# Sparse attention into two mixtures of experts on one core: local q and k loaded heads side by side and turned by 128-wide products, half of the strided v moved to GpSimd's queue

## The chip, the cores and the metric

The kernel runs on 1 core of one Trainium2 chip. The metric is the device time of one execution in microseconds, taken on that core. The median of 3 runs of the kernel before is 1208.98 us (1208.12 to 1211.52).

## What is computed

Three layers one after the other, in float32. Only the first is touched by the change. It is attention over 4 batches of 8 heads, 576 positions of 64 numbers each. Heads 0 to 3 look at the last 32 positions ("local"), heads 4 to 7 at the earlier positions of the same residue modulo 32 ("strided"):

```
scores = scale * np.matmul(q, k.transpose(0, 1, 3, 2))
rel = pos[:, None] - pos[None, :]
mask_local = (rel >= 0) & (rel < stride)
mask_strided = (rel >= 0) & (pos[None, :] % stride == pos[:, None] % stride)
masks = np.stack([mask_local if h < H // 2 else mask_strided for h in range(H)], axis=0)
...
attn = attn / (np.sum(attn, axis=-1, keepdims=True) + 1e-09)
return np.matmul(attn, v)
```

Its 2304 rows of 512 then go through a mixture of 8 experts with a fixed capacity of 288 rows each, and through a second one in which every row passes all 4 experts with given weights.

## The kernel before

`front` (L48) does the attention and the first router's logits; `experts` does the two mixtures and takes most of the time. In `front` the work of a batch is cut into 10 units: 5 strided ones (two groups of 6 or 7 residues times 18 positions each) and 5 local ones (blocks of 64 queries by 96 keys). Over the 4 batches these are 40 units. A loop over t (L374 on) works on several units at once, at a fixed distance: at step t the scores of unit t (`scores`, L186 strided, L189 local, both TensorE), the exponentials of t-1 (`exps`, L205, ScalarE), their normalisation for t-2 (`norm`, L213 and L214 on VectorE and the product L215 on GpSimd), the turning of the weights of t-4 (`tr_p`, L222 TensorE, then a copy by ScalarE into `pT`), and the product with v of t-5 (`av`, L235 strided from `vs`, L242 local from `vl`).

Before scores can be taken, q and k must have the head dimension on the partitions. `piece` does that, two pieces a step (`pre`), 16 pieces a batch. Strided pieces (L153) are four TensorE transposes of 72 rows into a PSUM tile `tr` and a copy into `qS` or `kS`. Local pieces (L164) are six products with the identity: three times t, two times x (the head of a pair), each with a 96x64 tile of `ql` or `kl` as the weights, the two heads written to partitions 0 to 63 and 64 to 127. One copy then moves 128x288 numbers to `qL` (VectorE and ScalarE by turns, scaled) or `kL` (VectorE); it reads PSUM in order and writes every sixth number of a row, because a partition of `ql` holds six consecutive positions. There are 8 local pieces a batch, 32 in all.

The order on each engine is the order in which the code is written; no scheduler moves it. `keep_busy` (L409) adds products of a constant tile in the first steps.

Loads go by SyncE's queue: at the start `load_qk(0)`, `load_v(0)`, `load_qk(1)` and `load_vl(0)`; then at each step t with t % 10 == 2 first `load_qk` of the batch after next and then `load_v` of the next batch, and at t % 10 == 6 `load_vl` of the next batch. `load_v` issues 13 transfers (L73) for the ten tiles of `vs`, `load_vl` five (L80, L82) for `vl`, `load_qk` one for each of `qs`, `ks`, `ql`, `kl` (L59, L62; the first batch has `qs` and `ks` in four slices). A transfer issued by SyncE waits until the one eight places earlier has landed, since eight semaphores go round. In the prologue GpSimd issues four small loads of its own (L110, L116, L119).

When the loop is over, `experts` writes the attention rows out (L282, L292), routes and gathers them, and runs its products.

Of the kernel before, what the change touches and what calls it, by code (L numbers as in the profile page):

```python
# [18 lines left out]
FT = mybir.dt.float32  # L19
# [15 lines left out]
def dap(t, off, *dims):  # L35
    return bass.AP(tensor=t.tensor, offset=t.offset + off, ap=[list(d) for d in dims])

def front(tc, ident, hot, q, k, v, wg, dp, xd, L, ready, hold, deferred):
    nc = tc.nc
    B, H, S, D = q.shape  # L40
    hs = S * D
    with ExitStack() as st:
        cst = st.enter_context(tc.tile_pool(name="fc", bufs=1))
        ld = st.enter_context(tc.tile_pool(name="fl", bufs=2))
# [6 lines left out]
        def load_qk(b, kinds="sl"):  # L51
            T = LD.setdefault(b, {})
            if "s" in kinds:
                for nm in ("qs", "ks"):
                    T[nm] = ld.tile([72, 32, 64], FT, name=nm)
            n = 8 if b == 0 else 32
            for r in range(0, 32 if "s" in kinds else 0, n):
                for nm, src in (("qs", q), ("ks", k)):
                    nc.sync.dma_start(T[nm][:, r:r + n].rearrange("p r d -> p (r d)"), dap(src, (b * H + 4) * hs + r * D, [hs, 4], [32 * D, 18], [1, n * D]))  # L59
            for nm, src in (("ql", q), ("kl", k)) if "l" in kinds else ():  # L60
                T[nm] = ld.tile([96, 4, 6, 64], FT, name=nm)
                nc.sync.dma_start(T[nm].rearrange("p h r d -> p h (r d)"), dap(src, b * H * hs, [6 * D, 96], [hs, 4], [1, 6 * D]))  # L62

        def load_v(b, lo=0, hi=10):
            T = LD[b]
            if not lo:
                T["vs"] = ld.tile([126, 10, 128], FT, name="vs")
            for t, (b0, n) in list(enumerate(zip(starts, sizes)))[lo:hi]:
                p = 0
                while p < n:  # L70
                    h, rp = divmod(b0 + p, 16)
                    m = min(n - p, 16 - rp)
                    nc.sync.dma_start(T["vs"][18 * p:18 * (p + m), t], dap(v, (b * H + 4 + h) * hs + 2 * rp * D, [2 * D, m], [32 * D, 18], [1, 2 * D]))  # L73
                    p += m

        def load_vl(b):
            T = LD[b]
            T["vl"] = ld.tile([96, 9, 256], FT, name="vl")
            nc.gpsimd.memset(T["vl"][:32, 0], 0.0)
            nc.sync.dma_start(T["vl"][32:, 0].rearrange("p (h d) -> p h d", d=D), dap(v, b * H * hs, [D, 64], [hs, 4], [1, D]))  # L80
            for h in range(4):
                nc.sync.dma_start(T["vl"][:, 1:, 64 * h:64 * h + 64], dap(v, (b * H + h) * hs + 32 * D, [D, 96], [64 * D, 8], [1, D]))  # L82

        load_qk(0)
        load_v(0, 0, 6)
        load_qk(1, "s")
        load_v(0, 6)
# [32 lines left out]
        units = []  # L120
# [7 lines left out]
        def copy(out, in_, scale=None, eng="p"):  # L128

            flip[0] += 1  # L130
            ch = side_of[eng]
            if ch == "a" or (ch == "f" and flip[0] % 2):
                if scale is None:
                    nc.scalar.copy(out, in_)
                else:
                    nc.scalar.activation(out, in_, AF.Copy, scale=scale)
            elif scale is None:
                nc.vector.tensor_copy(out, in_)
            else:
                nc.vector.tensor_scalar(out, in_, scale, None, op0=OP.mult)  # L140

        def piece(b, i):

            j, i = divmod(i, 8)
            p = ps.tile([128, 512], FT, name="tr", bufs=2)
            sc = 0.125 if j == 0 else None
            if i < 4:
                if i == 0:
                    (QS, KS)[j][b] = wk.tile([128, 4, 16, 18], FT, name=("qS", "kS")[j])
                src, dst = LD[b][("qs", "ks")[j]], (QS, KS)[j][b]  # L150
                for a in range(4):
                    r = 8 * i + 2 * a
                    nc.tensor.transpose(p[:, 72 * a:72 * a + 72], src[:, r:r + 2, :].rearrange("p r d -> p (r d)"), ident[:72, :72])  # L153
                copy(dst[:, :, 4 * i:4 * i + 4, :].rearrange("p h r j -> p r h j"), p[:, :288].rearrange("p (r h j) -> p r h j", r=4, h=4), sc, "q" if sc else "p")
            else:
                hp, a = divmod(i - 4, 2)
                if i == 4:
                    (QL, KL)[j][b] = wk.tile([128, 2, 576 + 32 * j], FT, name=("qL", "kL")[j])
                    if j:
                        nc.gpsimd.memset(KL[b][:, :, :32], 0.0)  # L160
                src, dst = LD[b][("ql", "kl")[j]], (QL, KL)[j][b]
                for t in range(3):
                    for x in range(2):
                        nc.tensor.matmul(p[64 * x:64 * x + 64, 96 * t:96 * t + 96], src[:, 2 * hp + x, 3 * a + t, :], ident[:96, :96], start=True, stop=True)  # L164
                copy(dst[:, hp, 32 * j:].rearrange("p (s a t) -> p a t s", a=2, t=3)[:, a], p[:, :288].rearrange("p (t s) -> p t s", t=3), sc, "q" if sc else "r")

        def shape(n):
            b, kind, g = units[n]
# [141 lines left out]
        def logits(n):  # L310
            b, kind, g = units[n]
            if kind or g not in (2, 4):
                return
            i0, m = (0, 128) if g == 2 else (128, 160)
            p = LP[n] = ps.tile([128, 512], FT, name="xr", bufs=2)
            for h in range(4):
                nc.tensor.matmul(p[32 * h:32 * h + 32, :m], wgs[:, h], XTS[b].rearrange("p h j r -> p h (j r)")[:, h, i0:i0 + m], start=True, stop=False)
            if n < N - 1:
                logits_local(n)
# [44 lines left out]
        p = ps.tile([128, 512], FT, name="pt")  # L364
# [9 lines left out]
        for t in range(N + 14):  # L374
            t_now[0] = t
            if t < N and t % 10 == 2 and units[t][0] + 1 < B:
                if units[t][0] + 2 < B:
                    load_qk(units[t][0] + 2)
                load_v(units[t][0] + 1)
                nxt = [(units[t][0] + 1, i) for i in ORDER]  # L380

            if t < N and t % 10 == 6 and units[t][0] + 1 < B:
                load_vl(units[t][0] + 1)
            if t == 28:
                side = cst.tile([128, 18, 8], FT, name="side")
                nc.gpsimd.memset(side, 0.0)
                nc.gpsimd.iota(side.bitcast(I32)[:, :, 4], pattern=[[1, 18]], base=0, channel_multiplier=18)
                rs = cst.tile([128, 18], FT, name="rs")
                nc.vector.tensor_reduce(rs, pr, AX.X, OP.add)
                nc.vector.tensor_scalar(rs, rs, 1e-9, None, op0=OP.add)  # L390
                nc.vector.reciprocal(rs, rs)
                nc.vector.tensor_tensor(side[:, :, :4], pr, rs[:, :, None].to_broadcast([128, 18, 4]), OP.mult)
                nc.gpsimd.dma_start(dap(xd, 512, [18 * XW, 128], [XW, 18], [1, 8]), side)
            if t % 10 == 6:
                todo += nxt
                nxt = []

            def at(d, f):
                if 0 <= t - d < N:
                    f(t - d)  # L400

            def pre():
                if todo and t:
                    piece(*todo.pop(0))

            def keep_busy(n):
                p = ps.tile([128, 512], FT, name="xr", bufs=2)
                for i in range(n):
                    nc.tensor.matmul(p, hot[:, :128], hot, start=True, stop=True)  # L409

            if BUSY[0] <= t < BUSY[1]:
                keep_busy(BUSY[2] + 2 * (t < 2))
            at(4, tr_p)
            if N < t < N + 5:
                keep_busy(2)
            at(2, norm)
            while late2:
                x = late2.pop(0)
                if x is None:
                    break  # L420
                x()
            while late:
                late.pop(0)()
            if t == N + 4:
                logits(N - 1)
            at(5, av)
            rows("o")
            if t < N:
                at(10, logits)
            elif t == N + 3:  # L430
                logits(N - 3)
            elif t == N + 5:
                logits_local(N - 1)
            pre()
            at(1, exps)
            rows("s")
            if t < N:
                scores(t)
            pre()
# [941 lines left out]
```

## Time and profile before

| what | value |
|---|---|
| median of 3 runs | 1208.98 us |
| the profiled execution, its own time | 1208.96 us |
| its span, first to last instruction | 1207.2 us |
| TensorE busy over the span | 1177.4 us (98%) |
| VectorE / ScalarE / GpSimd busy | 71% / 52% / 35% |
| the attention loop | about 11 to 125 us of the span |

The times of rows are microseconds from the span's start unless they say ns. A busy engine is not an engine at its peak: matmuls are pipelined and their ends are modelled. The share of the whole span says little about a change in the first tenth of it, so that tenth is read by itself below.

### The profile page before, as it was taken

The page shows a single profiled execution, that of the slowest core. Times are in us where ns is not written, and L with a number is a line of the kernel's source. Part 1 is how long each engine was busy: PE and PEld are TensorE (multiplying, and loading weights), DVE is VectorE, ACT ScalarE, POOL GpSimd, SP SyncE. Part 2 cuts the span into 40 slices and gives each one's busy share as a digit, 9 for nine tenths or more (in the row PEclk, how much of TensorE's full clock was granted, in tenths as well). Part 3 has the DMA queues.
Part 4 walks back from the last instruction along what each step waited for, and adds up shares of the span by engine and source line. Part 5 has one row for each costly group of instructions (what it writes and reads, how often), then busy time and mean ns, then how long its engine had stood idle before and what let it go on. Part 6 is the DMA issues. An engine that isn't in the chain of part 4 may idle for free.

```text
span 1207.2 us, 24909 instructions
## 1 busy us (share of the span) xinstructions
PE 1177.4 (98%) x9088; PEld 1038.6 (86%) x9095; DVE 853.9 (71%) x2248; ACT 621.8 (52%) x1602; POOL 422.9 (35%) x453
## 2 busy tenths in 40 slices
PE   9999799999999999999999999999999999999997
PEld 6777588898888888899999988999888999899996
DVE  5777677777785877778765588767877766766673
ACT  5898455542441442455545455555555555555552
POOL 4343030100000101001012565565755556756553
PEclk9999899999999999999999999999999999999999
DMA  8761564553252452475665433333433333333320
GB/s 187 181 151 39 172 203 147 163 166 99 88 160 81 136 156 56 141 226 170 191 204 156 127 90 102 98 100 102 125 103 89 105 105 105 123 106 102 98 81 36
DMA packets 191955, 152.98 MB, mean 127 GB/s; under 512 B 27640, under 2 KB 158776, under 8 KB 191400
## 3 DMA queue, kind: packets, MB, share of 16 engines
q1 hardware_dynamic: 188664, 141.74, 40.2%
q0 software_dynamic: 3168, 9.65, 2.5%
q8 instruction: 71, 1.16, 0.4%
q14 instruction: 52, 0.43, 0.1%
HBM read 141.77 MB, written 9.58 MB: 125 GB/s over the span
## 4 chain that ended last, share of the span: by engine, by line
PE 82%; DVE 7%; issue 3%; ACT 3%; DMA 2%; POOL 2%; SPq 0%; POOLq 0%; DVEq 0%; ACTq 0%
PE o L971 35%; PE h L971 18%; PE h L1201 16%; DVE wl L746 3%; DMA raw<-in_moe_w_dram 2%; PE tr L164 2%; PE pt L222 1%; PE pa L601 1%; PE tr L153 1%; PE av L242 1%; PE s L186 1%; PE av L235 1%; ACT hh L864 1%; POOL wl L1190 1%; DVE u L746 1%
## 5 line engine op out<-in xcount | busy, mean ns | idle before, releaser
L746 DVE TENSOR_TENSOR wl<-raw,wh 128x512 fp32r<-128x512 f32 x352 | 272.0, 804 | 4.6 <-ACT wh L844 3.8
L971 PE MATMUL o<-wl,hh 128*128 128x512 f32 x576 | 227.8, 395 | 0.0
L971 PE MATMUL o<-wh,hh 128*128 128x512 f32 x576 | 227.7, 395 | 0.0
L971 PE MATMUL o<-wh,hl 128*128 128x512 f32 x576 | 226.5, 393 | 0.0
L864 ACT ACTIVATE hh<-h 128x256 fp32r<-128x256 f32 (+1 forms) x208 | 81.7, 393 | 241.2 <-PE h L971 221.4
L844 ACT CAST wh<-raw 128x512 fp32r<-128x512 f32 x272 | 160.0, 619 | 59.8 <-DMA raw<-in_moe_w_dram 57.7
L1190 POOL TENSOR_TENSOR wl<-raw,wh 128x512 fp32r<-128x512 f32 x96 | 122.5, 1298 | 194.8 <-ACT wh L1189 194.7
L746 DVE SCALAR_TENSOR_TENSOR hl<-h,hh 128x256 fp32r<-128x256 f32 (+1 forms) x208 | 89.8, 432 | 103.6 <-ACT hh L864 102.4
L891 POOL DMA_INDIRECT xg<-xd,idx x24 | 26.3, 1095 | 367.0 <-DVE idx L746 285.0
L971 PEld LDWEIGHTS o<-wh,hl 128*128 128x128 f32 x576 | 108.6, 188 | 23.3
L1201 PE MATMUL h<-hold,wh 128*128 128x256 f32 x640 | 120.9, 282 | 1.4 <-DVE u L746 1.1
L1201 PEld LDWEIGHTS h<-hold,wh 128*128 128x128 f32 x640 | 107.9, 188 | 15.8 <-DVE u L746 2.8
L746 DVE SCALAR_TENSOR_TENSOR hl<-u,hh 128x256 fp32r<-128x256 f32 x144 | 83.0, 576 | 46.5 <-ACT hh L864 46.5
L1176 ACT CAST wh<-sums 128x512 fp32r<-128x512 f32 x96 | 59.8, 622 | 106.9 <-POOL sums L1164 70.6
L971 PEld LDWEIGHTS o<-wl,hh 128*128 128x128 f32 x576 | 108.6, 189 | 6.0
L971 PEld LDWEIGHTS o<-wh,hh 128*128 128x128 f32 x576 | 108.5, 188 | 6.1
L864 ACT ACTIVATE hh<-u 128x256 fp32r<-128x256 f32 x144 | 59.9, 416 | 103.3 <-DVE u L746 103.2
L746 DVE TENSOR_TENSOR u<-h,u 128x256 f32<-128x256 f32 x144 | 60.2, 418 | 62.9 <-PE h L1201 55.5
L746 DVE TENSOR_TENSOR wl<-sums,wh 128x512 fp32r<-128x512 f32 x96 | 74.7, 779 | 36.7 <-ACT wh L1176 36.7
L1201 PE MATMUL h<-hold,wl 128*128 128x256 f32 x320 | 89.8, 281 | 0.0
L971 PE MATMUL h<-xh,wh 128*128 128x288 f32 x256 | 76.1, 297 | 0.0
L971 PE MATMUL o<-hh,wl 128*128 128x288 f32 x256 | 76.0, 297 | 0.0
(271 smaller groups left out, 2927.2 us busy)
## 6 DMA issues: line engine op xcount, KB each, us to landing
raw<-in_moe_w_dram SPq DMA_DIRECT2D x464, 256.0 KB
vl<-in_v_dram SPq DMA_DIRECT2D x16, 192.0 KB
ql<-in_q_dram SPq DMA_DIRECT2D x4, 576.0 KB
kl<-in_k_dram SPq DMA_DIRECT2D x4, 576.0 KB
qs<-in_q_dram SPq DMA_DIRECT2D x3, 576.0 KB
ks<-in_k_dram SPq DMA_DIRECT2D x3, 576.0 KB
xd<-y SPq DMA_DIRECT2D x2, 576.0 KB
xd<-hl SPq DMA_DIRECT2D x5, 192.0 KB
```

What stands on the lines that cost most here:

```text
L153: nc.tensor.transpose(p[:, 72 * a:72 * a + 72], src[:, r:r + 2, :].rearrange("p r d -> p (r d)"), ident[:72, :72])
L164: nc.tensor.matmul(p[64 * x:64 * x + 64, 96 * t:96 * t + 96], src[:, 2 * hp + x, 3 * a + t, :], ident[:96, :96], start=True, stop=True)
L186: nc.tensor.matmul(out[:rows], lt, rt, start=True, stop=True)
L222: nc.tensor.transpose(p[:keys, rows * j:rows * j + rows], T["p"][:rows, j, :keys], ident[:rows, :rows])
L746: return f(*args, **kw)
L844: nc.scalar.copy(c["h"][:, sl], c["raw"][a])
L864: nc.scalar.activation(hi, src, AF.Relu)
L891: nc.gpsimd.indirect_dma_start(out=xg[:, k, :], out_offset=None, in_=xd, in_offset=bass.IndirectOffsetOnAxis(ap=idx[:, k:k + 1], axis=0))
L971: nc.tensor.matmul(out, a, b, start=start, stop=stop)
L1176: nc.scalar.copy(S["W"][nm][0], src[nm]())
L1190: nc.gpsimd.tensor_tensor(l, r, h.bitcast(FT), OP.subtract)
L1201: mmx = lambda o, a, b, first, lastm, n: (nc.tensor.matmul(o, a, b, start=first, stop=lastm, skip_group_check=True), tick(n / 2315 + 0.009))
```

## The change

Four edits, all in `front`:

- `ql` and `kl` are kept as position, head, dimension instead of head, position, dimension, so that the heads of one position lie side by side. Each is loaded by four transfers, one a head, of 96x6 pieces of 64 numbers (256 bytes) instead of one transfer of 96x4 pieces of 384 numbers (1536 bytes).
- A local piece is three products with 96x128 weights (two heads at once) instead of six with 96x64.
- Its copy runs through s first and t inside: it writes three neighbouring numbers, skips three, and reads PSUM in steps of 96 numbers.
- For batches 1 to 3, tiles 5 to 9 of `vs` (6 of the 13 transfers) are issued by GpSimd, and `load_v` stands before `load_qk`.

```
-                T[nm] = ld.tile([96, 4, 6, 64], FT, name=nm)
-                nc.sync.dma_start(T[nm].rearrange("p h r d -> p h (r d)"), dap(src, b * H * hs, [6 * D, 96], [hs, 4], [1, 6 * D]))
+                T[nm] = ld.tile([96, 6, 4, 64], FT, name=nm)
+                for h in range(4):
+                    nc.sync.dma_start(T[nm][:, :, h, :], dap(src, (b * H + h) * hs, [6 * D, 96], [D, 6], [1, D]))
...
-                    nc.sync.dma_start(T["vs"][18 * p:18 * (p + m), t], dap(v, (b * H + 4 + h) * hs + 2 * rp * D, [2 * D, m], [32 * D, 18], [1, 2 * D]))
+                    (nc.gpsimd if b and t > 4 else nc.sync).dma_start(T["vs"][18 * p:18 * (p + m), t], dap(v, (b * H + 4 + h) * hs + 2 * rp * D, [2 * D, m], [32 * D, 18], [1, 2 * D]))
...
-                    for x in range(2):
-                        nc.tensor.matmul(p[64 * x:64 * x + 64, 96 * t:96 * t + 96], src[:, 2 * hp + x, 3 * a + t, :], ident[:96, :96], start=True, stop=True)
-                copy(dst[:, hp, 32 * j:].rearrange("p (s a t) -> p a t s", a=2, t=3)[:, a], p[:, :288].rearrange("p (t s) -> p t s", t=3), sc, "q" if sc else "r")
+                    nc.tensor.matmul(p[:, 96 * t:96 * t + 96], src[:, 3 * a + t, 2 * hp:2 * hp + 2, :].rearrange("p h d -> p (h d)"), ident[:96, :96], start=True, stop=True)
+                copy(dst[:, hp, 32 * j:].rearrange("p (s a t) -> p a s t", a=2, t=3)[:, a], p[:, :288].rearrange("p (t s) -> p s t", t=3), sc, "q" if sc else "r")
...
+                load_v(units[t][0] + 1)
                 if units[t][0] + 2 < B:
                     load_qk(units[t][0] + 2)
-                load_v(units[t][0] + 1)
```

On TensorE, the step in which batch 1's first local unit meets v, where two pieces of batch 2 stand around the scores (`tr` is the PSUM tile of a piece, `pt` that of the turned weights, `av` that of the product with v); before:

```order
L340 MATMUL xr<-four,lg 128x16
L345 MATMUL xr<-four,lg 32x16
L242 MATMUL av<-pT,vl 64x64 x8
L164 MATMUL tr<-ident,ql 64x96 x6
L186 MATMUL s<-kS,qS 126x126 x4
L164 MATMUL tr<-ident,ql 64x96 x6
L222 MATMUL pt<-ident,pr 96x128 x4
L242 MATMUL av<-pT,vl 64x64 x8
```

And in the changed kernel:

```order
L340 MATMUL xr<-four,lg 128x16
L345 MATMUL xr<-four,lg 32x16
L242 MATMUL av<-pT,vl 64x64 x8
L164 MATMUL tr<-ident,ql 128x96 x3
L186 MATMUL s<-kS,qS 126x126 x4
L164 MATMUL tr<-ident,ql 128x96 x3
L222 MATMUL pt<-ident,pr 96x128 x4
L242 MATMUL av<-pT,vl 64x64 x8
```

Nothing has moved; the output of a piece's products is 128 partitions high as that of L222 is, and no longer 64 as that of L242 is.

On SyncE, from batch 1's `ks` to the first loads for batch 2; before:

```order
L59 DMA ks<-in_k_dram 72x2048
L73 DMA vs<-in_v_dram 108x1x128
L73 DMA vs<-in_v_dram 36x1x128
L73 DMA vs<-in_v_dram 72x1x128
L73 DMA vs<-in_v_dram 108x1x128 x2
L62 DMA ql<-in_q_dram 96x4x384
L62 DMA kl<-in_k_dram 96x4x384
L80 DMA vl<-in_v_dram 64x4x64
L82 DMA vl<-in_v_dram 96x8x64 x4
L59 DMA qs<-in_q_dram 72x2048
L59 DMA ks<-in_k_dram 72x2048
L62 DMA ql<-in_q_dram 96x4x384
```

And in the changed kernel:

```order
L59 DMA ks<-in_k_dram 72x2048
L74 DMA vs<-in_v_dram 108x1x128
L74 DMA vs<-in_v_dram 36x1x128
L74 DMA vs<-in_v_dram 72x1x128
L74 DMA vs<-in_v_dram 108x1x128 x2
L63 DMA ql<-in_q_dram 96x6x64 x4
L63 DMA kl<-in_k_dram 96x6x64 x4
L81 DMA vl<-in_v_dram 64x4x64
L83 DMA vl<-in_v_dram 96x8x64 x4
L74 DMA vs<-in_v_dram 126x1x128 x2
L74 DMA vs<-in_v_dram 36x1x128
L74 DMA vs<-in_v_dram 90x1x128
```

Ahead of `vl` of batch 0 there are now eight transfers where there were two (and as many more further up, for batch 0 itself); behind it comes `vs` of batch 1 before `qs` of batch 2.

On GpSimd, around the clearing of a `kL` tile, where a step with t % 10 == 2 begins; before:

```order
L215 TENSOR_TENSOR pr<-pr,r 128x2x96
L160 MEMSET kL 128x2x32
L215 TENSOR_TENSOR pr<-pr,r 126x4x126 x2
L215 TENSOR_TENSOR pr<-pr,r 108x4x108 x2
L79 MEMSET vl 32x256
```

And in the changed kernel:

```order
L215 TENSOR_TENSOR pr<-pr,r 128x2x96
L161 MEMSET kL 128x2x32
L74 DMA vs<-in_v_dram 108x1x128 x2
L74 DMA vs<-in_v_dram 36x1x128
L74 DMA vs<-in_v_dram 72x1x128
L74 DMA vs<-in_v_dram 108x1x128 x2
```

Six issues now stand ahead of the normalisation of the next batch's first unit.

## Rows read from the trace of the kernel before

**Rows 1.** Busy time by stage: length, engines (us, count), TensorE's granted clock, DMA share, GB/s.
```profile
20.00:118.00 98.00, 96.76 (x1563) 74.83 (x1562) 74.20 (x476) 87.61 (x389) 35.68 (x48) 1.00 0.61 136
...
126.00:140.00 14.00, 13.26 (x155) 10.59 (x153) 9.36 (x44) 10.23 (x27) 0.00 (x0) 0.88 0.62 178
140.00:160.00 20.00, 13.93 (x110) 9.29 (x107) 11.29 (x44) 7.31 (x16) 6.00 (x6) 0.83 0.74 216
```

**Rows 2.** Chain that ended last, 60 to 70 us: start, length (us), engine, tile, line.
```profile
63.57 0.40 PE tr L153 x4
63.97 0.44 PE pt L222 x4
...
64.70 0.61 PE av L242 x16
65.32 0.50 PE tr L164 x12
65.81 0.64 PE s L186 x8
66.45 0.65 PE tr L164 x12
67.10 0.57 PE pt L222 x4
```

**Rows 3.** Waits of SyncE's queue, 0 to 200 us: total, times, longest.
```profile
SPq L292 <- ACT hh L291: 27.8, 2, 26.8
...
SPq L80 <- DMA ks<-in_k_dram: 2.9, 1, 2.9
```

**Rows 4.** Instructions by group and shape, 0 to 130 us: busy, mean ns; idle before, releaser.
```profile
L138 DVE COPY kL<-tr 128x288 f32<-128x288 f32 x16 | 10.7, 671 | 1.4 <-PE tr L164 1.3
...
L340 PEld LDWEIGHTS xr<-four,lg 128*128 128x128 f32 x16 | 2.4, 190 | 0.9 <-DVE lg L138 0.8
...
L140 DVE TENSOR_SCALAR qS<-tr 128x288 f32<-128x288 f32 x5 | 2.2, 443 | 0.0
```

**Rows 5.** SyncE's queue in order of time, 4 to 56 us: start, length, line, transfer.
```profile
21.78 0.33 SPq L62 DMA_DIRECT2D kl<-in_k_dram  x1
25.01 0.69 SPq L80 DMA_DIRECT2D vl<-in_v_dram  x1
25.74 6.98 SPq L82 DMA_DIRECT2D vl<-in_v_dram  x4
...
52.31 2.33 SPq L82 DMA_DIRECT2D vl<-in_v_dram  x4
```

**Rows 6.** Transfers moved from 8 to 12 us, mostly 1536-byte packets: queue: packets, MB, engine share.
```profile
q1 hardware_dynamic: 643, 0.96, 107.5%
```

**Rows 7.** Transfers moved from 54 to 56 us, 256-byte packets of `vl`.
```profile
q1 hardware_dynamic: 1978, 0.50, 122.3%
```

**Rows 8.** Transfers moved from 27 to 35 us, while `vl` of batch 0 comes in.
```profile
DMA packets 3695, 1.47 MB, mean 184 GB/s; under 512 B 3405, under 2 KB 3671, under 8 KB 3671
```

**Rows 9.** TensorE in order of time: first use of `vl`, second use, a later turning.
```profile
35.53 0.69 PE L242 MATMUL av<-pT,vl 96*64 96x64 f32 x16
...
39.79 0.63 PE L242 MATMUL av<-pT,vl 96*64 96x64 f32 x14
...
75.89 0.65 PE L222 MATMUL pt<-ident,pr 126*126 126x126 f32 x4
```

**Rows 10.** GpSimd in order of time: start, length, line.
```profile
10.49 0.57 POOL L119 DMA_DIRECT2D dpr<-in_moe_domain_probs_dram  x1
17.02 1.03 POOL L215 TENSOR_TENSOR pr<-pr,r 126x504 f32<-126x504 f32 x1 [5.96 <-DVE r L214]
...
68.84 0.15 POOL L160 MEMSET kL<- 128x64 f32 x1
71.73 1.29 POOL L215 TENSOR_TENSOR pr<-pr,r 126x504 f32<-126x504 f32 x1 [2.74 <-ACT hold L134]
...
86.86 1.22 POOL L393 DMA_DIRECT2D xd<-side  x1 [1.86 <-DVE r L214]
```

## The prediction, made before the result was known

> **What bounds the kernel now.** The change lies in the attention loop, the first tenth of the span, so I read that stretch and not the shares of the whole. First the busy times by stage [rows 1]: from 20 to 118 us TensorE is busy 96.76 of 98.00 us at the full granted clock, ScalarE 87.61, VectorE 74.20, GpSimd 35.68. TensorE is the bound of the loop, and all waits of it that a faster other engine could remove come to at most 98.00 - 96.76 = 1.24 us. Next the chain that ended last, in a stretch with local pieces [rows 2]: it is an unbroken row of TensorE groups, one right behind the other, so a microsecond of TensorE work taken out of the loop shortens it by a microsecond. Then what hangs on the loop's end [rows 3]: SyncE's queue stands 26.8 us, from the last load to the first attention row copied at about 126 us, and everything of the experts follows that. So a shift of the loop's end passes on one for one.
>
> **The form of a tile has a price; the products of a piece have none to give.** [rows 2] has both sides of it. L222 behind L153, both 128 high on the output side, takes 0.44 us for four records of 128 columns: 0.11 us a record, 0.86 ns a column. L153 behind the 64-high L189 needs 4 x 72 x 0.86 = 0.25 us by that, and takes 0.40: 0.15 us is the change of form. The same L164 takes 0.50 us behind L242 (also 64 high) and 0.65 behind L186: again 0.15. L222 takes 0.57 behind L164 and 0.44 behind L153: 0.13.
>
> A piece has 12 records of 96 columns (six products, two passes each). One after another they would need 12 x 96 x 0.86 = 0.99 us; they take 0.50. So the two heads of a pair already run side by side in the two halves of the array. The new piece has three products of two passes: 6 x 96 x 0.86 = 0.50 us. **The products gain nothing**, though half of the instructions go.
>
> What does change is the neighbours. I counted them in the order of TensorE's instructions, for all 32 pieces:
>
> - ahead of a piece: 16 times L186, 64 rows deep, a change of form before and after: 0. 9 times L242, no change before, one after: 9 x 0.15 = +1.35 us. 7 times a 128-high group (L409, L287, L276, L222), a change before, none after: 7 x 0.15 = -1.05.
> - behind a piece: 14 times L186: 0. 12 times L222: 12 x 0.13 = -1.56. 6 times another 128-high group: 6 x 0.13 = -0.78.
>
> The sum is 1.35 - 1.05 - 1.56 - 0.78 = -2.04 us, all of it in the loop's chain. From below: the waits of TensorE that shorter copies can take away, 1.24 us at most, so -3.3. From above: the weights of a piece are now 128 wide. L340, the one 128-wide product of two passes here, loads its weights in 190 ns a time (16 loads for 8 products) [rows 4]; were a pass held to that, a piece would need 6 x 0.19 = 1.14 us, +20 us in all. The nearer row is L153, also with 128-wide weights, whose steps of 0.25 / 4 = 0.06 us leave the loads hidden [rows 2]; I take 0.
>
> **The copies.** Those of the local pieces, 288 numbers written every sixth place, take 671 ns on VectorE for `kL` [rows 4]; of the 32 VectorE does 25 and ScalarE 7. The copy of a strided piece, as many numbers in long runs, takes 443 on VectorE. Runs of three lie between; I take 550. That frees 32 x 0.12 = 3.8 us of the two engines, for neither of which the loop waits; their cover is TensorE's chain. I take 0 for the time, and keep the 1.24 us of above as the other end.
>
> The new copy also reads PSUM in steps of 96 numbers, which no copy before does. The Trainium skill (SBUF — State Buffer, "Door 1: The DMA port swizzle") says that SBUF has lines of 16 bytes and PSUM of 8, and that accesses which go to a new line each time pay; for PSUM it says so of matmuls. By its first half runs of three beat single numbers, as 443 against 671 suggests; were its second half true of copies too, the reading would get slower, since each number now comes from another line.
>
> **The loads of ql and kl.** 1536-byte packets: from 8 to 12 us 643 packets at 107.5% of 16 engines [rows 6], so 1.075 x 16 x 4 / 643 = 107 ns each, 0.96 MB in 4 us or 240 GB/s. 256-byte packets: 1978 at 122.3% in 2 us [rows 7], 19.8 ns each, 250 GB/s. A batch's `ql` and `kl` are 768 packets now and 4608 then: 768 x 107 / 16 = 5.1 us and 4608 x 19.8 / 16 = 5.7 us. So the engines need 0.6 us more a batch.
>
> The trace shows no loss in bytes a second for the small packets. The Trainium skill (DMA: Bandwidth & Descriptors, "Why small descriptors are slow (HBM only)") speaks against the change here: a fixed 3 cycles a packet, so 11 cycles for 256 bytes where the data needs 8. An estimate by that page is 5.1 x (11/8) / (51/48) = 6.6 us a batch, 1.5 more than now; the rows say 0.6.
>
> SyncE issues six more transfers a batch. Four `vl` transfers of the same kind take 2.33 us where nothing holds them [rows 5], some 0.6 each; six are 3.6 us. The one consumer close behind is batch 0's `vl`: first issue at 25.01 us, issued over 7.7 us [rows 5], its 3328 packets moved between 27 and 35 us [rows 8], first read at 35.53 us [rows 9]. That first unit needs the block-0 transfer and heads 0 and 1, 1792 of the 3328: in at 27 + 8 x 0.54 = 31.3, some 2 us to land, so about 2 us to spare. The rest is read from 39.79 on. Ahead of it stand two sets of `ql` and `kl`, so up to 2 x 3.6 = 7.2 us of issue. Much of this falls into waits that are there anyway: `vl` stands from 22.1 to 25.0 behind the landing of batch 1's `ks`, and the eight `vs` before batch 1's `qs` take 10.27 us. I put its first issue at 29 to 30 us. Then the q and k packets are already gone and 1792 packets need 1792 x 19.8 / 16 = 2.2 us, with some 2 us to land: 33 to 35 us, still before 35.53. I take a stall of 0, and 0 to 5 us as its range. Batch 1's `vl` is issued by 54.6 [rows 5] and first read at 64.70 [rows 2], some 8 us to spare, and later batches are like it.
>
> **GpSimd's queue.** Six issues a batch, by the prologue's rows 0.57 us each, at worst 1.22 [rows 10]: 3.4 to 7.3 us. In batch 1 they lie in the idle time from 11.1 to 17.0 us. In batch 3 they start at 69.0 and end at 72.4 to 76.3, where the normalisation queued behind them now starts at 71.73. Its reader L222 starts at 75.89 [rows 9]. With 0.57 it ends at 73.7, and TensorE doesn't see it; with 1.22 TensorE stands some 1.7 us, and as much in batch 2. I take 0; bound 3.4. "v first" lets `vs` go before the waits of `qs` and `ql` for free buffers; nobody waits for that now: 0.
>
> **Sum.** -2.0 us. The profiled execution took 1208.96 us, the median is 1208.98; so 1207.0 us. About 0.3% (3.6 us) is what a measurement of this kernel can tell from no change; this is within it.
>
> **Rivals.**
>
> - *Late vl.* If the issues don't fall into waits and packets are slower among others, batch 0's `vl` comes 2 x (3.6 + 0.6) = 8.4 us later than now, against those 2 us to spare: TensorE stands up to 6.4 us at the first L242, 1207.0 + 6.4 = 1213.4, slower. It is slower by over 3.6 us from a stall of 5.6 us on. For it speaks that 1.47 MB in 8 us, 184 GB/s, move in that stretch already [rows 8]; against it, that they carry the same bytes. Short of that point, stalls of 1 to 5 us give 1208 to 1212.
> - *Slow copies.* VectorE is busy 74.20 of 98, so a step of 2.5 us leaves it some 0.6. Two `kL` copies a step could each grow by 0.3, to 0.97 us, unseen. At 1.2 us each, 8 steps lose 2 x 0.23: +3.7, so 1210.7, no measurable change. No copy in [rows 4] costs that.
> - *More than the sum.* All 1.24 us of waits go, and the loop's earlier end puts less of the following work into the stretches at a lower granted clock (0.88 and 0.83 on the mean, 126 to 160 us [rows 1]), where up to 20 x 0.17 = 3.4 us are lost: 1207.0 - 1.2 - 2 = 1203.8, faster.
> - *128-wide weights set the pace*: +20 us, 1227, if loads aren't hidden.
> - *The change doesn't do what it says*: the products stay at 0.50 us a piece. That is my forecast.
>
> **How the numbers follow.** Forecast 1207.0: 0.56. More than the sum: 0.15. Late `vl`: 0.17, of it 0.07 beyond 3.6 us. Slow copies: 0.09. Wide weights: 0.03. So faster 0.15, slower 0.07 + 0.03 = 0.10, same 0.75. The range leaves out the wide weights and the outer halves of the two end cases: 1203.5 to 1211.5.
>
> **What would show it.** L164 as 6 records in about 0.50 us behind L242 plus 0.15, and L222 behind it at 0.44 instead of 0.57; a loop that ends 2 us earlier; copies of `kL` near 550 ns; L242's first start at 35 us, or a wait for `vl` in front of it. I am wrong if L164 takes 0.25 us (then -8 us more), if TensorE waits for `vl`, `pr` or `tr`, or if copies go over 1 us.

## The result and the profile after

| kernel | median, us | range, us | ratio to before, 95% interval |
|---|---|---|---|
| before | 1209.66 | 1207.01 to 1212.43 (20 runs) | |
| after | 1216.36 | 1214.00 to 1231.66 (20 runs) | 1.0073 [1.0051, 1.0096] |

The change makes the kernel slower, by 0.5 to 1.0%, and its runs spread more. The ratio is not that of the two medians: these stand 0.55% apart, the means (1218.7 and 1209.6 us) 0.75%, since three runs of after lie above 1228. One run in this study, 1224.7 us of a kernel with transposes, lies over 1.5% above the fastest of its kernel and is left out of that kernel's ratio. The profiled execution of after took 1220.85 us, 11.9 more than that of before (1208.96). Much of the spread goes with TensorE's granted clock (its share of 2.4 GHz, as a mean over the run). The 89 runs of before beside the experiments have mean clocks from 0.996 (median 1207.2 us) to 0.990 (1212.4) and one of 0.989, some 0.9 us for each 0.001. So two comparisons are given where it matters: of medians, and of the runs with the same mean clock. At 0.993 before has 1209.7 us (23 runs) and after 1215.6 (6 runs): 5.9 us more at the same mean clock.

Busy times by stage of after, as in [rows 1]: length, engines (us, count), granted clock, DMA share, GB/s.
```profile
20.00:118.00 98.00, 95.90 (x1245) 77.62 (x1248) 64.80 (x428) 78.55 (x349) 38.82 (x55) 0.95 0.69 139
126.00:140.00 14.00, 11.87 (x126) 7.83 (x128) 7.84 (x34) 5.57 (x18) 0.51 (x1) 0.88 0.11 32
140.00:160.00 20.00, 15.45 (x184) 10.71 (x182) 12.47 (x62) 9.78 (x25) 2.40 (x3) 0.83 0.75 220
```
Two things differ in the first row: TensorE is a little less busy (95.90 us against 96.76), and its clock is 0.95 on the mean where it was 1.00. Its chain of work in the steady part of the loop, as in [rows 2]:
```profile
70.72 0.44 PE pt L222 x4
...
71.46 0.61 PE av L242 x16
72.07 0.84 PE tr L164 x6
72.91 0.64 PE s L186 x8
73.55 0.84 PE tr L164 x6
74.39 0.44 PE pt L222 x4
```
The chain is still unbroken TensorE work. L222 behind L164 has come down from 0.57 to 0.44, as forecast; but L164 has gone up, to 0.84 us from 0.50 or 0.65, with half of the records. The first use of `vl`, as in [rows 9] (start, length, and the wait ahead with its releaser), and SyncE's queue ahead of it, as in [rows 5]:
```profile
35.14 0.61 PE L222 MATMUL pt<-ident,pr 128*96 128x128 f32 x4
35.82 0.45 PE L242 MATMUL av<-pT,vl 96*64 96x64 f32 x8
36.78 0.33 PE L242 MATMUL av<-pT,vl 96*64 96x64 f32 x2 [0.51 <-DMA vl<-in_v_dram]
37.84 0.69 PE L242 MATMUL av<-pT,vl 96*64 96x64 f32 x6 [0.73 <-DMA vl<-in_v_dram]
38.46 1.09 PE L287 MATMUL xr<-ident,hold 128*96 128x128 f32 x4
39.34 1.43 PE L164 MATMUL tr<-ident,ql 96*128 96x96 f32 x6
```
```profile
18.71 0.36 SPq L59 DMA_DIRECT2D ks<-in_k_dram  x1
19.11 3.81 SPq L74 DMA_DIRECT2D vs<-in_v_dram  x5
22.96 5.88 SPq L63 DMA_DIRECT2D ql<-in_q_dram  x4
28.88 2.80 SPq L63 DMA_DIRECT2D kl<-in_k_dram  x4
31.72 0.63 SPq L81 DMA_DIRECT2D vl<-in_v_dram  x1
32.40 3.04 SPq L83 DMA_DIRECT2D vl<-in_v_dram  x4
```
`vl` is issued from 31.72 us on, 6.7 later than in [rows 5]. TensorE's first unit of L242 takes from 35.82 to 38.46 us, 2.6 us in place of some 0.65: about 2.0 us are lost, 1.24 of them (0.51 + 0.73) as waits for `vl`. What stands behind it is slow as well: L287 takes 1.09 us and L164 1.43, where it takes 0.84 later. The windows say why:
```profile
37.00:48.00 11.00, 10.27 (x66) 8.80 (x64) 3.46 (x14) 4.26 (x18) 3.21 (x6) 0.53 0.66 155
48.00:58.00 10.00, 10.00 (x120) 8.37 (x119) 6.52 (x37) 6.79 (x31) 4.72 (x7) 1.00 1.21 194
```
From 37.3 to 47.5 us the granted clock is at its lower level (0.5, 1.2 GHz), from the second of the two waits on, and then back at 1.00 (2.4 GHz): 10.2 us. The same place of the loop, L242 at 64.70 in [rows 2], comes at 71.46 here, 6.8 us later. So of the profiled execution's 11.9 us, 6.8 are lost by then: 2.0 at the first L242, and 4.8 that the half clock and the slower pieces make together. The experts' first matmuls start at 156.14 us where before has 146.31, so 9.8 of the 11.9 lie ahead of them.

### The profile page after: what moved, and what is told of

Read it like the earlier page. It is cut to its first block, busy times and chain, and to the rows that moved or that the text cites. A ratio compares the mean times of both kernels' runs of the same rounds, so it can differ in the third digit from the quotient of the medians.

```text
span 1219.1 us, 24576 instructions
## 1 busy us (share of the span) xinstructions
PE 1187.3 (97%) x8897; PEld 1050.7 (86%) x8903; DVE 851.2 (70%) x2248; ACT 620.5 (51%) x1602; POOL 433.8 (36%) x471
## 4 chain that ended last, share of the span: by engine, by line
PE 81%; DVE 6%; DMA 3%; issue 3%; ACT 2%; POOL 2%; SPq 2%; POOLq 0%; DVEq 0%; ACTq 0%
PE o L971 35%; PE h L971 19%; PE h L1201 16%; DVE wl L746 2%; PE tr L164 2%; DMA raw<-in_moe_w_dram 1%; PE pa L601 1%; DMA ks<-in_k_dram 1%; PE pt L222 1%; PE av L242 1%; PE s L186 1%; POOL wl L1190 1%; DVE u L746 1%; SPq L63 1%; DVE acc L746 1%
```

## Experiments

All times are medians; "before" beside them is 1209.5, 1209.7, 1208.8 and 1210.1 us in the four groups of runs. A dash stands for before, a plus for the experiment, unless the text says that it edits after. The edits are shown shortened: W stands for the weights of a product, `...` for what is left out.

**The order of the loads: after, with batch 0's `vl` ahead of batch 1's `ql` and `kl`.**
```diff
-        load_qk(1, "l")
         load_vl(0)
+        load_qk(1, "l")
```


> The changed kernel, with the v tiles of batch 0's local heads loaded ahead of batch 1's ql and kl instead of behind them. Theory 'late vl': in the changed kernel TensorE stood about 2 us before and inside its first L242 (35.8 to 38.5 us), waiting for vl, and its granted clock was at the lower level from about 37.6 to 47.8 us, some 5 us lost in the profiled execution. Without the wait the first L242 starts at about 35.5 us, no stretch of low clock follows, and the executions above 1217 us go: about 1213.5 us, and a narrow spread. Theory 'wide products alone': the wait is noise and all of the loss is in the pieces; then it stays at 1216 us. If ql and kl of batch 1 now come late instead, a wait stands in front of L164 near 37 us.

Measured: 1214.94, ratio 1.0052 [1.0035, 1.007], runs from 1213.8 to 1216.7. TensorE waits for no transfer, and its clock stays up through the loop:
```profile
20.00:126.00 106.00, 104.34 (x1464) 82.60 (x1465) 72.56 (x476) 87.96 (x390) 42.59 (x59) 1.00 0.61 128
```
So the wait and the half clock behind it are gone in this profile, and none of the six runs is as long as after's longest (up to 1231), but most of the loss of the median stays. At a mean clock of 0.993 it is 1214.6 (2 runs), 4.9 above before. Of this, 3.3 us lie ahead of the experts' first matmuls in the profile (before: 146.31):
```profile
149.65 5.75 PE L1314 MATMUL h<-hot 128*128 128x512 bf16 x15 [0.33 <-issue]
```
No transfer is waited for up to there, so this is mostly the pieces. But the edits of v are still in this kernel, and alone they cost something too (below); what the pieces take of the 4.9 us is not shown by this run.

**What a record of the new products costs: after, each product cut in two of 48 columns.** The same columns in all, with twice the records and weight loads.
```diff
-  matmul(p[:, 96*t : 96*t+96], W, ident[:96, :96])
+  for u in range(2):
+      matmul(p[:, 96*t+48*u : 96*t+48*u+48], W, ident[:96, 48*u : 48*u+48])
```


> The changed kernel with each 128-wide product of a local piece cut into two of 48 columns. In the changed kernel the records of L164 follow each other by 112 ns, where 96 columns need 82. Theory 'weights': the load of 128 columns of weights in two passes sets the step, whatever the columns of the product: 12 records at 112 ns, a piece 1.34 us and its change of form, 32 x 0.67 = 21 us more than the changed kernel, about 1238 us. Theory 'columns': a wide record costs 1.16 ns a column: 12 records at 56 ns, a piece as in the changed kernel, about 1216 us.

Measured: 1249.64, one run. Its chain of work (L165 is after's L164):
```profile
74.88 0.62 PE av L243 x16
75.50 1.47 PE tr L165 x12
76.96 0.64 PE s L187 x8
```
Six more records and no more columns: 1.47 - 0.84 = 0.63 us more, 0.105 a record. In the trace the starts of the records follow each other by 112 ns, as they do at 96 columns. So the columns don't set the step; each pass of a 128-wide product has its price of 112 ns, and theory "weights" stands. The records of the weight loads fit it (count, shortest/median/longest in ns, first and last start), in after from 60 to 120 us and in before:
```profile
L164 PEld LDWEIGHTS tr<-ident,ql x48: 186/192/192, 72.0 to 107.9; 96*128 96x128 f32 x48
L164 PEld LDWEIGHTS tr<-ident,ql x192: 132/137/138, 13.6 to 98.6; 96*64 96x64 f32 x192
```
A load takes 192 ns in place of 137; loads overlap, so the step is shorter than a load. The time went 12 us past its 1238, in a stretch late in the loop (windows 20 to 110 and 110 to 145 us), at half clock with no wait ahead of it:
```profile
20.00:110.00 90.00, 89.54 (x1168) 75.46 (x1169) 53.53 (x347) 65.22 (x288) 34.40 (x48) 1.00 0.74 151
110.00:145.00 35.00, 35.00 (x246) 30.47 (x246) 11.77 (x76) 13.80 (x59) 5.49 (x7) 0.51 0.00 1
```

**Transposes: after, with the same tiles turned by transposes.**
```diff
-  nc.tensor.matmul(p[...], W, ident[:96, :96], start=True, stop=True)
+  nc.tensor.transpose(p[...], W, ident[:96, :96])
```


> The changed kernel with the local pieces turned by TensorE's transpose (one pass) instead of a product with the identity (two passes); loads as in the changed kernel. A record of 96 columns should take 82 ns as for the other transposes (0.86 ns a column), so a piece 0.25 + 0.15 = 0.40 us against 0.84 in the changed kernel and 0.50 to 0.65 before. 'Late vl' says that the gain is partly lost: the loop reaches the first L242 some 3.5 us earlier, at about 32 us, and vl of batch 0 still comes at 37 to 38, so TensorE stands about 5 us there, and the low clock follows: 1203 to 1210 us. If vl were no matter, 32 x 0.44 = 14 us come off: 1202 us.

Measured: 1211.59, ratio 1.0022 [1.0007, 1.0036]. The piece does shrink, and a new wait, with some 13.7 us of half clock behind it (29.4 to 43.1 us), takes back much of the gain (the wait of TensorE for a transfer, up to 120 us):
```profile
PE tr L154 <- DMA ks<-in_k_dram: 2.1, 1, 2.1
```

**Transposes and `vl` first.** Both edits together.

> Both edits: transposes for the local pieces, and vl of batch 0 ahead of batch 1's ql and kl. By both theories together 32 x 0.44 = 14 us from the pieces and 2.5 us from the wait: about 1200 us, 9 us or 0.8% below the kernel before. If ScalarE, at 0.89 of the loop, becomes the bound, or ql and kl of batch 1 come late, less: 1200 to 1205 us.

Measured: 1211.07, ratio 1.0014 [1.0001, 1.0027]; 1200 was expected. A piece in the chain, and the windows 20 to 43 and 43 to 118 us:
```profile
67.97 0.40 PE tr L164 x3
68.37 0.66 PE s L186 x8
```
```profile
20.00:43.00 23.00, 21.35 (x219) 16.38 (x218) 11.94 (x78) 16.94 (x72) 6.28 (x8) 0.70 0.76 167
43.00:118.00 75.00, 74.11 (x1119) 57.20 (x1119) 59.44 (x393) 69.95 (x316) 36.38 (x51) 1.00 0.67 131
```
Three records of one pass take 0.40 us, and follow each other by 83 ns, 0.87 ns a column, with weights as wide as after's; a load of these weights takes 140 ns. So it is the two-pass product that pays 112 ns, not the width alone. But the faster loop now meets batch 1's `ks`, waits 1.5 us for it at 27.6 us, and then has 13.7 us at half clock. The one run with a mean clock of 0.993 took 1206.8 us; the runs around the median had 0.986 and 0.987.

**The loads alone: before, with the side by side tiles and four loads a tensor; products 64 wide.**
```diff
-  T[nm] = ld.tile([96, 4, 6, 64]); one dma_start of [96][4][6 * D]
+  T[nm] = ld.tile([96, 6, 4, 64]); for h in range(4): dma_start of [96][6][D]
```


> The kernel before, with one part of the change: the local q and k tiles with the heads side by side, loaded by four transfers a tensor; products stay 64 wide, copies and v as before. Theory 'late vl': SP's queue gets six more issues in the prologue, the first vl issue moves from 25.0 to about 31.7 us as it did in the changed kernel, and the first L242 (at 35.0 to 35.8 us) waits some 2 us for vl; if TensorE's granted clock then stays at 1.00 the time is about 1211, if it falls to half for some 10 us as in the changed kernel's profile (10.2 us at half, so 5.1 lost) about 1214 to 1217. Rival 'the loads are free, the products are the whole loss': 1209.5, within 1 us, and no wait for vl on TensorE.

Measured: 1215.96, ratio 1.0075 [1.0042, 1.0108], runs from 1210.9 to 1227.0. In the profiled run (1211.7):
```profile
PE av L243 <- DMA vl<-in_v_dram: 1.1, 2, 0.7
PE av L236 <- DMA vs<-in_v_dram: 0.6, 2, 0.4
```
The loads alone make the wait and the spread. The second wait, for batch 2's `vs` at 80 to 83 us, is not in after's profile: there v stands ahead of the next q and k, and half of it on GpSimd's queue. In this run the clock stayed at 1.00 from 20 to 118 us, so that no half clock follows the waits; of the ten runs the two at a mean clock of 0.993 took 1211.3, 1.6 above before, and the five at 0.988 and below took 1217.6 to 1227.0. So the waits cost some 1.6 us by themselves, and the long runs are up to 15 us longer at a lower clock. No trace of a long run was kept: that half clock behind a wait makes them too is argued from after's profile.

**The copies alone: before, with the copies in runs.**
```diff
-  dst "p (s a t) -> p a t s" <- p "p (t s) -> p t s"
+  dst "p (s a t) -> p a s t" <- p "p (t s) -> p s t"
```


> The kernel before, with one part of the change: the copies out of a local piece write in runs and read with a stride, all else as before. In the changed kernel these copies took 460 ns on VectorE and 472 on ScalarE against 670 and 686 before, so 32 copies save some 6.8 us between two engines. Theory: none of it shows, TensorE's chain holds the loop: 1209.5, within 1 us. Rival 'the copies hold the chain at places': TensorE waited 0.7 us in 68 for kL's copies, so up to 1 to 2 us faster: 1207.5 to 1208.5.

Measured: 1210.01, ratio 1.0003 [0.9991, 1.0015]. No change, as expected. In its profile the experts' first matmuls do start 1.4 us earlier, at 144.87 us, but nothing of it is left at the end.

**The v loads: before, with half of the later strided v by GpSimd's queue and v first (both), or by GpSimd's queue alone.**
```diff
-  nc.sync.dma_start(T["vs"]...)
+  (nc.gpsimd if b and t > 4 else nc.sync).dma_start(T["vs"]...)
...
+  load_v(b + 1)      # in the first of the two alone
   load_qk(b + 2)
-  load_v(b + 1)
```


> The kernel before, with one part of the change: half of the later strided v by GpSimd's queue, and v ahead of the next q and k in the loop. The theory is that it costs nothing: GpSimd issues six transfers of 0.62 us each (3.7 us) three times where nobody waits for it, so 1209.5, within 1 us, no DMA wait on TensorE over 0.5 us. Rival 'v too early': the six first transfers land at 14 to 18 us, 0.35 MB ahead of batch 1's qs and ks, and push these back by 0.35 MB at some 200 GB/s, 1.7 us, so that L153 waits for ks at 27 us: up to 1211.

> The kernel before with half of the later strided v by GpSimd's queue, but v still behind the next q and k in the loop. With both edits of v the median was 1214.7, and TensorE's first L242 waited 0.6 us for vl, whose first issue had moved from 25.0 to 27.9 us. Theory 'early transfers': the six transfers that GpSimd issues from 11 us on share the DMA engines with batch 0's loads, SP's issues of the first v tiles stretch from about 7 to 11 us and vl is late by itself, whatever the order in the loop: a wait for vl of 0.5 to 1.2 us remains, 1212 to 1215. Rival 'order': the loss came from v(1) standing ahead of batch 2's q and k: no wait for vl, 1209.5 within 1 us.

Measured: both 1214.72, ratio 1.0035 [1.0018, 1.0053]; the queue alone 1211.89, ratio 1.0035 [1.0012, 1.0058]. The first has a wait for `vl` of 0.6 us, with `vl` issued at 27.9 us instead of 25.0. In the second `vl` is issued at 27.1 us, so the early transfers do delay it, but its profile has no wait for a transfer at all, and a clock of 0.76 from 126 to 140 us, where before had 0.88. Neither theory holds as put: a loss is there without the order, and a wait for `vl` is not seen in the second. The forecast of "no cost" is wrong for both. Whether the order adds to the loss is not settled: at mean clocks of 0.990 and 0.991 the median is 1215.1 with both edits (5 runs), 1212.7 with the queue alone (4) and 1212.2 for before (8). What carries the loss to the end stays open.

**Order by need: after with transposes, `qs` and `ks` of batch 1 and `vl` of batch 0 early, v of batch 1 by SyncE alone.**
```diff
-  load_v(0, 0, 6); load_qk(1, "s"); load_v(0, 6); load_qk(1, "l"); load_vl(0)
+  load_v(0, 0, 4); load_qk(1, "s"); load_v(0, 4); load_vl(0); load_qk(1, "l")
-  nc.gpsimd if b and t > 4 else nc.sync
+  nc.gpsimd if b > 1 and t > 4 else nc.sync
```


> The changed kernel with three edits: the products of a local piece are transposes (three records of one pass and 0.41 to 0.47 us in place of six in 0.84), the prologue's order is q and k of batch 0, four tiles of its v, qs and ks of batch 1, the rest of v, vl, then ql and kl of batch 1, and batch 1's v stays on SP's queue. With the transposes alone and vl first TensorE waited 4.1 us for batch 1's ks and then ran 13.7 us at half clock (6.8 us lost): 1211. Theory 'order': here 0.35 MB less and 0.12 MB later stand ahead of ks, it lands 2 us sooner, TensorE does not wait over 0.5 us for a transfer before 45 us, its clock stays up between 29 and 43 us, and the time is 1199 to 1203. Rival 'the clock falls anyway': with less work in the pieces the granted clock falls somewhere in the first 60 us without such a wait, and the time is 1207 to 1211.

Measured: 1213.85, ratio 1.0055 [1.0032, 1.0078], slower than without. Up to 50 us it does nearly what the theory says: the clock is 1.00, and the one wait for a transfer is 0.65 us, for batch 1's `ql` at 34.8 us (the theory allowed 0.5). The 4.1 us that the expectation names as the wait for `ks` with both edits is 1.5 us in the profile above. Then batch 2's `qs` and `ks`, issued at 45.6 us behind all of batch 1's v, are late:
```profile
51.78 0.47 PE L154 MATMUL tr<-ident,qs 72*128 72x72 f32 x4 [1.70 <-DMA qs<-in_q_dram]
...
54.81 0.74 PE L154 MATMUL tr<-ident,ks 72*128 72x72 f32 x4 [2.07 <-DMA ks<-in_k_dram]
```
and half clock follows from 53.4 to 67.1 us. The late transfer has only moved by a batch. The queues are full around it: the DMA share is 1.12 from 30 to 40 us, and 1.07 from 50 to 58. From 38 to 46 us, ahead of these issues, it is 0.36, so it is not the bytes alone but also when they are issued.

**New form in batches 2 and 3 alone.** Batches 0 and 1 load and turn as before, v is loaded as before, copies go in runs; with after's products, and with transposes.
```diff
   for x in range(2 if b < 2 else 0): matmul(... 64 wide, as before)
+  if b > 1: matmul(... 128 wide)       # or transpose(...)
```


> As the kernel with the new form in batches 2 and 3 alone, but with the changed kernel's 128-wide products in place of transposes. Theory 'pieces': each of 16 pieces costs 0.84 in place of 0.65 us, 3.0 us, less half of the form changes of 2.0, so 2.0 us slower than before with the same spread of runs and no wait for vl: 1211 to 1212. Rival 'all of the loss is late transfers': 1209.5 or a little faster, 1208.5.

> The kernel before, with heads side by side and transposes (three records, one pass) for the local q and k of batches 2 and 3 alone, the copies in runs, and all loads of v as before: batches 0 and 1 load and turn as before. Theory 'the loss of the transposes was in the first 60 us': no transfer is late, because the loads of the first two batches are those of before; 16 pieces take about 0.35 to 0.45 us in place of 0.65 and half of the form changes go (2.0 / 2 us), so 16 x 0.25 + 1 = 5 us faster if the granted clock holds: 1203 to 1206. Rival 'the clock takes it back': TensorE's granted clock falls for some us more than before once the pieces are shorter, and the time is 1208 to 1211 with a mean clock of 0.988 or less.

Measured: products 1212.35, ratio 1.0039 [1.0025, 1.0054], and no wait for a transfer above 0.2 us: the pieces' cost once more, without the edits of v, though with four loads a tensor in two batches. Its pieces take 0.84 us each in the chain. At a mean clock of 0.992 it is 1212.2 us (2 runs) where before has 1210.6 (18): 1.6 for the 2.0 expected. In its profile the experts' first matmuls start at 148.81 us, 2.5 later than in before. Transposes 1208.63 (all 12 runs; 1208.1 without the longest), ratio 1.0013 [0.9991, 1.0034], with runs from 1204.5 to 1224.7. Here batch 2's v is late, the very transfer that the change puts first:
```profile
PE av L242 <- DMA vs<-in_v_dram: 1.3, 2, 0.9
```

**The same with transposes, and v first and half by GpSimd from batch 2 on.**
```diff
-  nc.sync.dma_start(T["vs"]...)
+  (nc.gpsimd if b > 1 and t > 4 else nc.sync).dma_start(T["vs"]...)
-  load_qk(b + 2); load_v(b + 1)
+  b == 0: load_qk(2, "s"); load_v(1); load_qk(2, "l")
+  b >= 1: load_v(b + 1); load_qk(b + 2)
```


> The kernel with heads side by side and transposes in batches 2 and 3 alone, where TensorE waited 1.3 us for batch 2's v (issued from 74 us on, read at 77.6), with the change's own remedy for that: v ahead of the next q and k, half of it by GpSimd's queue, from batch 2 on; and behind batch 2's qs and ks for batch 1's v, so that the first 60 us load as before. Theory 'late transfers': no DMA wait over 0.5 us on TensorE up to 130 us; the median falls from 1208.6 to 1203 to 1206, with no runs above 1212. Rival 'the clock takes it back': no wait either, but a mean clock of 0.990 or less in half of the runs, and a median of 1208 to 1211.

Measured: 1208.57, ratio 0.9985 [0.9971, 0.9999], runs from 1205.2 to 1212.7. It is the only one whose ratio lies below 1, by 0.15%, and the only one with transposes that has no wait for a transfer. Its median missed the theory's 1203 to 1206 and lies where the rival put it, but not for the rival's reason: two of the 12 runs, not half, have a mean clock of 0.990 or less. The row where the experts' first matmuls start, of this kernel and of before:
```profile
142.23 5.84 PE L1323 MATMUL h<-hot 128*128 128x512 bf16 x16
```
```profile
146.31 5.41 PE L1314 MATMUL h<-hot 128*128 128x512 bf16 x15 [0.33 <-issue]
```
The loop, up to this row, is 4.1 us shorter, near the 5 that were forecast for the pieces; the copies alone showed 1.4 of it in their profile. The spans are 1207.4 and 1207.2 us: what comes after takes 4.3 us more in this profile. In the 14 profiles of this study that rest takes from 1060.9 us (before) to 1065.2 us (this one), with no order by the loop's length, so one profile a kernel can't say what a shorter loop does to it. From 150 to 160 us the clock is 0.83 against 0.98, and from 180 to 200 us TensorE is busy 18.75 us against 19.84. The median keeps 1.6 of the 4.1. How much of it always goes back, and by what, is not settled.

## Why the prediction was wrong, step by step

The forecast was 1207.0 us with no measurable change most likely; the result is slower, above the range. By its own steps:

- **TensorE bounds the loop, and the loop's end passes on one for one.** The first half is right: the chain of after is unbroken TensorE work between the waits. The second is not shown. A longer loop made a longer kernel (9.8 us up to the experts' first matmuls and 11.9 in all in after's profile), but of the 4.1 us of the last experiment the median kept 1.6, and the rest behind the loop varies by 4.3 us from profile to profile.
- **The form of a tile.** Right where it can be read: L222 behind L164 took 0.44. L164 takes 0.84 behind L242 and behind L186 alike, and 0.64 behind the 128-high L409, so the price ahead of a piece was paid where it was put, with some 0.2 us for the 0.15 taken.
- **"The products gain nothing", with hidden weight loads.** This step failed. The piece was to take 0.50 us, or 0.65 with the change of form; it takes 0.84, so 0.19 more for each of 32 pieces: +6.1 us in place of 0, and with the -2.0 of the neighbours, which no run took by itself, +4.1. With `vl` first the experts' first matmuls start 3.3 us later in the profile, and the kernel takes 4.9 more at equal clock. The row I took for the price of a 128-wide load, L153 with 0.06 us a step, was a transpose of one pass, whose weight loads take 140 ns against L340's 190 in the same trace; after's products have two passes. Transposes of these tiles step by 83 ns, their products by 112, whatever the columns. The rival "128-wide weights set the pace" was the right mechanism. Its 190 ns is what a load lasts (192 in after), but the records follow each other by 112, so its price was too high (it would have made 1227), and its chance of 0.03 was too low. The Trainium skill (TensorE: Matmul & The Clock Gate, "LDWEIGHTS (loading the stationary operand)") gives a load's time as its columns divided by 1.2, so 107 ns for 128. For the two-pass products the step of 112 ns agrees with it, though a load's own record lasts 192; the transposes, with weights as wide, step by less (83, and some 63 for L154's 72 columns).
- **The loads: bytes a second.** Right: from 27 to 35 us after moves 6016 packets at a share of 92.8%, so 0.928 x 16 x 8 / 6016 = 19.7 ns each; 19.8 was taken.
- **The loads: batch 0's `vl`.** This step failed too. Its first issue was put at 29 to 30 us and the stall at 0; the issue came at 31.7 and the first L242 lost 2.0, 1.24 of it as waits. The sum for it was short in two places: `ql` and `kl` of batch 1 took 5.9 + 2.8 = 8.7 us to issue, where 0.6 each was taken for eight, and the needed heads landed some 4 us behind their issue. The rival "Late vl" named the mechanism, and its lower half, stalls of 1 to 5 us, is what happened.
- **What the prediction had no step for: the clock behind a wait.** It counted a stall as its own length. In the profiled run 10.2 us at half clock begin in the wait, and the runs with a low mean clock are the long ones. This bears on the spread of after (up to 1231) more than on its median: with the wait taken away the median falls by 1.4 us and the longest run by 15.
- **The copies.** 550 ns were taken; `kL`'s take 460, near the 443 of long runs, and are worth nothing, as forecast. The doubt drawn from the Trainium skill (SBUF — State Buffer, "Door 1: The DMA port swizzle"), that reading PSUM in steps might get slower, is not borne out: writing in runs of three and reading in steps of 96 numbers together cost these 17 ns. (Of PSUM the page speaks for matmuls alone.)
- **GpSimd's queue.** The issues took 0.62 us each (0.57 taken) and no engine waits for them. But the part alone costs 0.35%, where 0 was forecast. I had counted the issues, and not that the first six transfers go out at 11 to 16 us among batch 0's loads. They do move the issue of `vl` from 25.0 to 27.1 us; that this is the reason of the loss is argued, not shown.

The parts don't add up to the whole: the loads alone cost 0.75%, the change with `vl` first 0.52, the v loads 0.35, and the whole change 0.73. The loads and the v loads delay the same transfer (`vl` is issued at 31.1, 27.9 and, with both, 31.7 us, where before has 25.0), and the clock's part is not a sum of theirs.

## What to carry to other kernels

Price a TensorE instruction by a row of the same kind: passes, width and mode; a transpose says nothing of a two-pass product, and the change's own tiles with transposes were 0.44 us a piece cheaper than with products. Count the issues of a queue by what the same transfers take when the queue is loaded, and ask of each transfer how long before its first reader it lands; a loop that gets faster makes late what was in time. Price a wait of the bounding engine by its length and by what the granted clock may do behind it.

## What the runs showed of the hardware

- Two-pass float32 products with 128-wide weights follow each other by 112 ns at 96 columns and at 48; two 64-wide ones side by side by 83 ns at 96 columns; transposes of the same 128-wide tiles by 83 as well.
- The loads of 128-wide float32 weights for two-pass products last 192 ns, those of 64-wide ones 137, and those of 128-wide ones for a transpose 140.
- Waits of 0.5 + 0.7 us went with 10.2 us at half clock in one run, and waits of 0.7 + 0.4 us with none in another (the loads alone); waits of 1.5 us and of 1.7 + 2.1 us were followed by 13.7 and 13.6. With the 48-column products 34 us at half clock came without any wait ahead. Runs of one kernel differ by up to 20 us, the long ones with the low mean clocks.
- 256-byte packets moved as many bytes a second as 1536-byte ones, but a tensor in four transfers cost SyncE 2.8 to 6.5 us of issue in after, in place of one issue of 0.3 to 1.4 in before.
